# Reordering the turn from batch 0 to batch 1 in a Strassen MLP behind block-recurrent attention: what VectorE and ScalarE do first

## The chip, the cores and the metric

The kernel runs on one core of a Trainium2 chip. The metric is device time in microseconds, as the median of several executions; lower is better. A profile of one execution shows every instruction of five engines: TensorE (PE, its weight loads PEld), VectorE (DVE), ScalarE (ACT), GpSimd (POOL) and SyncE (SP), which issues the transfers (DMA). Each engine works through its own list of instructions in the order of the program; the order is written by hand here, and the waits between engines follow from the data and the buffers.

## The reference

Two parts, all in fp32. First attention between a sequence and a small state, for 8 batches and 8 heads of width 64; then an MLP with a quick GELU on all 8 x 544 tokens.

```python
B, H, S, Ns, D = 8, 8, 512, 32, 64
scores = scale * x @ state.T                 # (B, H, S, Ns); scale = 1/sqrt(D)
xread  = softmax(scores) @ state             # x reads the state
scores2 = scale * state @ x.T                # (B, H, Ns, S)
sread  = softmax(scores2) @ x                # the state reads x
y = concat([xread, sread], axis=2)           # (B, H, S + Ns, D) -> (4352 tokens, 512)
h = y @ w_in                                 # 512 -> 2048
g = h / (1 + exp(-1.702 * h))
out = g @ w_out                              # 2048 -> 512
```

## The kernel before

The inputs x and the weights come as 64-bit words, and the kernel turns the weights into fp32 itself, 128 rows at a time (a row block: 16 of w_in, then 16 of w_out): a mask on VectorE, a clamp of the exponent by two activations on ScalarE, then four more operations on VectorE. ScalarE's clamp for later row blocks is asked for ahead (`powers_to`).

```python
def round_a(i):                      # mask (DVE, L216) and clamp
    if i not in power: mask(i)
    ...
    nc.scalar.activation(out=sc.bitcast(FP32), in_=sc, func=AF.Relu, bias=edge[0], scale=-8.0)   # L227
    nc.scalar.activation(out=sc, in_=sc.bitcast(FP32), func=AF.Relu, bias=edge[1], scale=-1.0)   # L228

def round_b(i, ahead, follows):      # needs the clamp of i
    nc.vector.scalar_tensor_tensor(sc, hi, -0x80000000, sc, ...)                                 # L245
    powers_to(ahead)
    nc.vector.scalar_tensor_tensor(dst, lo, 2.0**-32, dst.bitcast(I32), ALU.mult, ALU.add)       # L248
    if follows and i + 1 in raw: fraction(i + 1)                                                 # L234
    nc.vector.scalar_tensor_tensor(dst, dst, 2.0**-20, sc.bitcast(FP32), ALU.mult, ALU.mult)     # L252

def round_to(n, ahead=AHEAD):
        ...
        round_b(i, min(i + 1 + ahead, i + 2 if i >= nin else nin), ...)   # nin = 16: from there on w_out
```

The down-projection (g @ w_out) is done by Strassen's scheme in Winograd's form: seven products P1 to P7 in place of eight, at the cost of sums of blocks. The sums of the left side are S1 = A21 + A22, S2 = S1 - A11, S4 = A12 - S2 and S3 = A11 - A21; those of the right side (the weights) are T1 = B12 - B11, T2 = B22 - T1, T4 = B21 - T2 and T3 = B22 - B12. For batch 0 this runs while w_out is still arriving, a loop over 8 pairs of row blocks, with the rest of batch 1's up-projection (`up_x`) between:

```python
rest = list(range(2 * nper, NF))         # f = 8 .. 15 of batch 1's up-projection
for i in range(HF):                      # HF = 8
    round_to(nin + 2 * i + 2)
    if i == 0:
        pair(i, "P1", "P2")
        for b in (1, 0):
            for g in range(NG):
                att_eT(b, g)             # four transposes on PE into two banks, copied by ACT
        round_to(nin + 4)
        att_sread(1); att_sread(0)       # the states' reads
        att_M(1, 2, True); att_M(1, 3)
        ...
        pair_sums(i)
        att_srT(0); att_srT(1)
        ps7["P4"], up_bank = (psH.tile(...) for k in (4, "up"))
    else:
        pair_sums(i); pair(i, "P1", "P2")
    if i > 1:
        up_x(1, rest.pop(0), bank=up_bank)      # matmuls, then the gelu on ACT (L549)
    late()                                      # P6 P5 P7 P3 P4 of pair i
    if i == HF // 2:
        load_state(2); load_x_squares(2)
```

Behind the loop come the sums for the batches 1 to 7. These use Strassen's scheme twice: each of the products (256 x 1024 by 1024 x 256) of the outer level is made of seven smaller ones, so every weight block needs sums of its own (three, `low_sums`) and one in place (`low_third`). The sums of three blocks are kept in SBUF in turn (`low_made`), all are stored in DRAM (`low_keep`) and loaded again for later batches. `low_away` makes them in a passing room (tag xT, one buffer) and stores them.

```python
def low_sums(t, rooms):                  # each step needs the one before
    return [(T_of, v) for v in ((t1, b12, b11), (t2, b22, t1), (t4, b21, t2))]

low_away(6, B22)
low_made(5, T1, 1)
for u in range(NU - 2): s12(1, u, S)     # S1, S2 of batch 1, two of four quarters
                                         # batch 0's epilogue: 7 additions, out by DMA
nc.scalar.copy(k1, ps7["P1"]); tt(osb, ps7["P2"], k1, ALU.add); ...
for f in rest:                           # f = 14, 15
    up_x(1, f, bank=up_bank)
...                                      # two copies on ACT: the T2, T4 of pairs 0 to 3
s12(1, NU - 2, S)
low_third(T1)
for u in range(NU - 1): s3(1, u, S)
low_away(3, T3); low_third(T3)
turn_x(2)                                # four 32x32 transposes of batch 2's x
low_made(2, T2, 0)
s12(1, NU - 1, S); s3(1, NU - 1, S)
for b in range(1, B):
    ...
    ahead = {"P1a": [(low_third, (B22,)), (low_third, (T2,)), (low_away, (4, T4)), (low_third, (T4,))]}   # b == 1
    ...
    strassen_two(b, out_of(b), hooks, a4)
```

In `strassen_two` hooks with names run between the products; for batch 1 P1 and P2 are plain, and P5, P6, P3, P7, P4 are the two-level ones:

```python
product(bank(0), A_of(0, 0), B11, "P1"); nc.scalar.copy(k1, bank(0))       # hooks P1a, P1b after each half
for i in range(3):
    sums1[i](); sums2[i]()               # VectorE: sums of S1, of S2
third_of(S1)
product(bank(1), A_of(0, 1), B21, "P2"); tt(osb, bank(1), k1)              # hooks P2a, P2b; bank(1) = bank_o[1]
first = {...: s4(u) at P5.1, .2, .5, .6; third_of(S2) at P5.3}             # for later batches sums2 too
strassen_low(left_of(S1, *r), (T1 ...), [h0, h1, bank_o[1]], p5, at)       # P5

def strassen_low(left, right, bank, R, at):       # x, y, z are the three banks
    product(x, a11, b11, True); nc.scalar.copy(y, x);     at(1)   # L700
    product(z, s1, t1, True);   nc.scalar.copy(c22, z);   at(2)   # L703
    product(y, s2, t2);         nc.scalar.copy(c12, y);   at(3)   # L706
    product(x, a12, b21);       nc.scalar.copy(c11, x);   at(4)   # L709
    product(y, a21, t3);        add(c22, y, c22);         at(5)   # L696
    product(z, s4, b22);        add(c12, z, c12);         at(6)
    product(y, a22, t4);        nc.scalar.copy(c21, y);   at(7)   # L718
```

At batch 1 the hooks P2a and P2b also hold the start of batch 2's attention: scores, two products with w_in (`att_M`), two transposes and two maxima on VectorE (P2a), and the two exps on ScalarE (`att_s_exp`, P2b), which write to the room with the tag xT.

Of the kernel before, what the change touches and what calls it, by code (L numbers as in the profile page):

```python
# [20 lines left out]
def kernel(  # L21
# [71 lines left out]
    def att_ps(shape, name):  # L93
        return psA.tile(shape, FP32, tag="att", name=name)
# [142 lines left out]
    def round_b(i, ahead, follows):  # L237


        if i not in begun:  # L240
            fraction(i)
        dst = begun.pop(i)
        lo, hi = words(i)
        sc = power.pop(i)
        nc.vector.scalar_tensor_tensor(sc, hi, -0x80000000, sc, ALU.bitwise_and, ALU.bitwise_or)  # L245
        powers_to(ahead)

        nc.vector.scalar_tensor_tensor(dst, lo, 2.0**-32, dst.bitcast(I32), ALU.mult, ALU.add)  # L248
        del raw[i]
        if follows and i + 1 in raw:  # L250
            fraction(i + 1)
        nc.vector.scalar_tensor_tensor(dst, dst, 2.0**-20, sc.bitcast(FP32), ALU.mult, ALU.mult)  # L252
# [19 lines left out]
    def round_to(n, ahead=AHEAD):  # L272

        nin = NFC * NPR
        while done["b"] < min(n, len(PIECES)):
            i = done["b"]
            powers_to(i + 1)
            round_b(i, min(i + 1 + ahead, i + 2 if i >= nin else nin), i >= nin or i + 1 < nin and (i + 1 < n or i >= NPR))
            done["b"] += 1
            while done["b"] > NPR and done["load"] < len(PIECES) and before(done["load"]) < done["b"]:  # L280
                load_weights(done["load"] + 1)
# [183 lines left out]
    def att_M(b, c, spare=False, banks=None):  # L465

        m = mpool.tile([P, NG, FC], FP32, tag=f"M{turns['M'] % NFC if b < 2 else c}", name=f"M_{b}_{c}")
        turns["M"] += 1
        A[b]["M", c] = m
        name = f"M_{b}_{c}_"  # L470
        ps = banks or [
            psH.tile([P, FC], FP32, tag="h", name=name + str(g)) if spare else att_ps([P, FC], name + str(g)) for g in range(NG)
        ]
        by_state(b, ps, lambda rows, j: w_in[c][rows, j])
        for g in range(NG):
            nc.scalar.copy(m[:, g], ps[g])  # L476
# [16 lines left out]
        t = A[b]["eT"][:, g].rearrange("p c q -> p (c q)")  # L493
        nc.vector.transpose(t, t)

    def att_eT(b, g):

        a = A[b]
        if g == 0:
            a["eT"] = apool.tile([P, NG, SCH, P], FP32, tag="e1" if b else "eT", name=f"eT_{b}")  # L500
        ps = att_ps([P, SCH, P], f"eT_{b}_{g}")
        for c in range(SCH):
            nc.tensor.transpose(ps[:, c], a["e2"][g][0][:, P * c : P * (c + 1)], ident)
        nc.scalar.copy(a["eT"][:, g], ps)
# [216 lines left out]
    def strassen_two(key, dst, hooks, a4):  # L721
# [129 lines left out]
        if key == 1:  # L851
            for i in range(3):
                sums1[i]()
                sums2[i]()
            third_of(S1)
            product(bank(1), A_of(0, 1), B21, "P2")
            tt(osb, bank(1), k1)
        else:
            o, h0, h1 = low_banks()
            own2 = {2: sums1[:1], 4: sums1[1:2], 5: sums1[2:], 6: [lambda: third_of(S1)]}  # L860
            lowly("P2", left2, B21, low_a, [h0, o, h1], osb, own2)
            low_load(2, 0)
            tt(osb, osb, k1)
# [6 lines left out]
        hook("P2")  # L870
        first = {i + 1: [lambda u=u: s4(u)] for i, u in zip((0, 1, 4, 5), range(NU))}
        first[3] = [lambda: third_of(S2)]
        if key > 1:
            first[1].insert(0, sums2[0])
            first[2].append(sums2[1])
            first[4] = sums2[2:]
        o, h0, h1 = low_banks()

        def at(i):
# [403 lines left out]
    def low_made(k, t, i):  # L1283

        for fn, args in low_sums(t, (low_a, low_b)[i]):
            fn(*args)
        low_keep(k, turn_rooms[i])
# [49 lines left out]
    def pair(i, *names):  # L1337

        f = ORDER[i]
        a11, a12, a21, a22 = a_of(f)  # L1340
        s1, s2, s4 = s_of(i) if i >= 0 and names[0] not in ("P1", "P2") else (None,) * 3
        t = t24(i) if s1 is not None else None
        for name in names:
            lhs, rhs = {
                "P1": lambda: (a11, B11[:, f]),
                "P2": lambda: (a12, B21[:, f]),
                "P5": lambda: (s1, T1[:, f]),
                "P6": lambda: (s2, t[:, 0]),
                "P7": lambda: (a21, B12[:, f]),
                "P3": lambda: (s4, B22[:, f]),  # L1350
                "P4": lambda: (a22, t[:, 1]),
            }[name]()
            for r in range(2):
                nc.tensor.matmul(  # L1354
                    ps7[name][:, HN * r : HN * (r + 1)], lhs[:, P * r : P * (r + 1)], rhs,
                    start=(i == 0 and r == 0), stop=(i == HF - 1), skip_group_check=True,
                )

    def late():

        pair(i, "P6", "P5", "P7", "P3", "P4")
        if i % 2:
            u = ORDER[i] // 2
            free.append(G.pop((0, u)))
            G.pop((0, HF // 2 + u))

    rest = list(range(2 * nper, NF))
    for i in range(HF):
        round_to(nin + 2 * i + 2)
        if i == 0:  # L1370
            pair(i, "P1", "P2")
            for b in (1, 0):
                for g in range(NG):
                    att_eT(b, g)
            round_to(nin + 4)
            att_sread(1)
            att_sread(0)
            att_M(1, 2, True)
            att_M(1, 3)
            t_room.append(pieces(apool.tile([P, NG, SCH * P], FP32, tag="eT", name="t_room_1"), 2, 2))  # L1380
            s4_room = pieces(apool.tile([P, NG, NB * Ns], FP32, tag="e1", name="s4_room"), 2, 2)
            pair_sums(i)
            att_srT(0)
            att_srT(1)
            ps7["P7"], ps7["P3"] = (att_ps([P, FC], f"down_{k}") for k in (7, 3))
            ps7["P4"], up_bank = (psH.tile([P, FC], FP32, tag="h", name=f"down_{k}") for k in (4, "up"))
# [4 lines that stand above are left out]
            up_x(1, rest.pop(0), bank=up_bank)  # L1391
        late()
        if i == HF // 2:
            load_state(2)
            load_x_squares(2)

    low_away(6, B22)
    low_made(5, T1, 1)
    for u in range(NU - 2):
        s12(1, u, S)  # L1400

    k1, k2, t01, k3 = (v[:, j] for v in (s_room, s4_room) for j in range(2))
    osb = opool.tile([P, 2, HN], FP32, tag="osb", name="osb_0_00")
# [7 lines left out]
    tt(osb, ps7["P2"], k1, ALU.add)  # L1411
    put_out(0, 0, osb)
    tt(k2, ps7["P6"], k1, ALU.add)
    tt(t01, ps7["P5"], k2, ALU.add)
    tt(k3, ps7["P7"], k2, ALU.add)
    tt(k1, ps7["P7"], t01, ALU.add)
# [2 lines left out]
    put_out(0, 1, t01)  # L1419
    tt(k3, ps7["P4"], k3, ALU.add)  # L1420
    put_out(1, 0, k3)
    for f in rest:
        up_x(1, f, bank=up_bank)
    for i, t in enumerate(t_room):
        nc.scalar.copy(sums[:, 2, 2 * S * i : 2 * S * (i + 1)], t.rearrange("p n k t -> p (n k t)"))
    s12(1, NU - 2, S)
    low_third(T1)
    for u in range(NU - 1):
        s3(1, u, S)
    low_away(3, T3)  # L1430
    low_third(T3)
    turn_x(2)
    low_made(2, T2, 0)
    s12(1, NU - 1, S)
    s3(1, NU - 1, S)

    for b in range(1, B):
        if b > 1:
            ahead = {"P1.1": [(up_strassen(b, S, *parts_x(b), A[b]["sums"]), ())]}
            if b == 2:  # L1440
                ahead["P1.5"] = [low_sums(B21, low_a)[2], (low_keep, (1, turn_rooms[0]))]
                ahead["P1.6"] = [(low_third, (B21,))]
        else:
            ahead = {
                "P1a": [(low_third, (B22,)), (low_third, (T2,)), (low_away, (4, T4)), (low_third, (T4,))]
            }
        if b + 1 < B:
            hooks = hooks_next(b + 1)
        else:

            steps, left, right = sr_sums()
            order = (
                ("P5.6", 2), ("P6.1", 3), ("P6.3", 6), ("P6.4", 7), ("P7.5", 8), ("P7.6", 9), ("P4.1", 16, 17), ("P4.5", 18, 19),
            )
            hooks = {name: [steps[i] for i in n] for name, *n in order}
            hooks["P3.7"] = [(low_third, (T1,))]
            beside = steps[10:16] + [(low_third, (t,)) for t in (B11, B21, T2, T3, T4, B22)]
            ahead["P2.1"] = [steps[i] for i in (0, 1)]
            ahead["P2.3"] = [steps[i] for i in (4, 5)]
        for name, first in ahead.items():  # L1460
            hooks[name] = first + hooks.get(name, [])
        a4 = {}

        at = hooks.setdefault("run", [])
        k = 3 if b + 1 < B else 0
        at[k:k] = [(low4_load, (a4,))]
        strassen_two(b, out_of(b), hooks, a4)
        if b + 2 < B:
            load_state(b + 2)
            load_x_squares(b + 2)  # L1470
# [35 lines left out]
```

## Time and profile before

| | |
|---|---|
| median of 3 runs | 710.29 us (709.15 to 710.42) |
| span in the profile | 708.5 us |
| TensorE busy | 684.5 us (97%) |
| VectorE busy | 573.5 us (81%) |
| ScalarE busy | 321.1 us (45%) |
| HBM traffic | 86.5 MB, 122 GB/s over the span |

In the profile an instruction appears with its engine, the line of the kernel, what it writes and reads (names of the program), and the idle time of its engine before it with what ended that. fp32 matmuls appear as two records each. A busy share is an average over all stages: the stage in which the engine stood still has to be looked up by its time. The part that matters here lies between 60 and 215 us: the loop over pairs to about 145, the turn from batch 0 to batch 1 to about 182 (the end of P5), and the other products of batch 1 to 211.

### The profile page before, as it was taken

How to read it: one execution, taken by the hardware profiler on the slowest of the kernel's cores; microseconds unless marked ns; L12 is line 12 of the kernel's file. 1: busy time of each engine (PE TensorE's matmuls, PEld its weight loads, DVE VectorE, ACT ScalarE, POOL GpSimd, SP SyncE). 2: the span in 40 equal slices, each digit the busy share in tenths (PEclk: the TensorE clock that was granted, in tenths of full speed). 3: DMA queues.
4: the chain of work that ended last, by engine and by line, in shares of the span. 5: the costliest groups of instructions: out<-in, count | busy, mean ns of one | idle time of the engine just before them, and what ended most of it. 6: DMA issues, size and time to landing. Idle time of an engine off the chain costs nothing.

```text
span 708.5 us, 13782 instructions
## 1 busy us (share of the span) xinstructions
PE 684.5 (97%) x5357; PEld 580.1 (82%) x5359; DVE 573.5 (81%) x1226; ACT 321.1 (45%) x704; POOL 0.8 (0%) x8
## 2 busy tenths in 40 slices
PE   7989999995999999999999999999999999999996
PEld 3433587773998799889999889889988998999995
DVE  6999979999697979697869887888878895887540
ACT  5687833313236543555346433652375336512420
POOL 0000000000000000000000000000000000000000
PEclk9999999997999999999999999999999999999999
DMA  8921326154525285516641474237433640241001
GB/s 224 369 80 63 106 91 148 63 192 150 163 76 124 81 262 150 109 35 194 204 105 34 128 247 125 42 107 237 148 65 105 211 149 31 59 144 66 16 1 31
DMA packets 106321, 87.41 MB, mean 123 GB/s; under 512 B 64784, under 2 KB 85776, under 8 KB 106256
## 3 DMA queue, kind: packets, MB, share of 16 engines
q1 hardware_dynamic: 106256, 86.53, 41.7%
q8 instruction: 43, 0.70, 0.4%
q14 instruction: 22, 0.18, 0.1%
HBM read 68.94 MB, written 17.56 MB: 122 GB/s over the span
## 4 chain that ended last, share of the span: by engine, by line
PE 85%; DVE 8%; ACT 3%; DMA 2%; issue 1%; SPq 0%; DVEq 0%; ACTq 0%
PE low L691 27%; PE o L691 15%; PE o L1111 13%; PE upx L1111 5%; PE h L546 5%; PE M L329 4%; PE o L1354 3%; PE o L588 2%; PE down L1354 2%; PE upw L1111 2%; PE o L329 1%; PE down_up L546 1%; PE sr L517 1%; PE warm L127 1%; DVE low L1281 1%; PE upx_sr L1111 1%
## 5 line engine op out<-in xcount | busy, mean ns | idle before, releaser
L691 PE MATMUL low<-w_out,g 128*128 128x128 f32 x416 | 54.3, 276 | 0.0
L691 PEld LDWEIGHTS low<-w_out,g 128*128 128x128 f32 x416 | 50.5, 192 | 4.5 <-issue 3.4
L1111 PE MATMUL o<-ta,M 128*128 128x256 f32 x192 | 49.9, 382 | 0.0
L1111 PE MATMUL upx<-aT,M 128*128 128x256 f32 x192 | 49.3, 379 | 0.0
L691 PE MATMUL low<-low,g 128*128 128x128 f32 x336 | 43.3, 275 | 0.0
L691 PEld LDWEIGHTS low<-low,g 128*128 128x128 f32 x336 | 40.3, 192 | 0.1
L1111 PEld LDWEIGHTS o<-ta,M 128*128 128x128 f32 x192 | 35.5, 190 | 6.0 <-ACT g L1157 1.6
L1111 PEld LDWEIGHTS upx<-aT,M 128*128 128x128 f32 x192 | 36.0, 190 | 4.6
L691 PE MATMUL low<-sums,later 128*128 128x128 f32 x280 | 36.1, 276 | 0.0
L1117 ACT ACTIVATE g<-o 128x512 f32<-128x512 f32 (+1 forms) x56 | 31.3, 559 | 10.2 <-PE o L1111 10.2
L476 ACT COPY M<-M 128x512 f32<-128x512 f32 x59 | 30.7, 597 | 11.6 <-PE M L329 11.6
L691 PEld LDWEIGHTS low<-sums,later 128*128 128x128 f32 x280 | 34.0, 194 | 0.1
L329 PE MATMUL M<-w_in,stT 64*32 64x512 f32 x472 | 31.9, 594 | 0.0
L1111 PE MATMUL o<-ta,ms 128*128 128x256 f32 x120 | 30.8, 379 | 0.0
L546 PE MATMUL h<-aT,M 128*128 128x512 f32 x64 | 28.7, 599 | 1.4 <-ACT M L476 1.4
L691 PE MATMUL o<-low,spare_M 128*128 128x128 f32 x160 | 22.2, 283 | 8.1 <-DVE osb L747 8.1
L227 ACT ACTIVATE low<-low,edge 128x512 f32<-128x512 int32 x30 | 21.6, 719 | 13.9 <-DVE low L216 13.8
L1117 ACT ACTIVATE g<-g 128x512 f32<-128x512 f32 (+1 forms) x28 | 16.8, 600 | 23.4 <-DVE g L1120 23.4
L691 PEld LDWEIGHTS o<-low,spare_M 128*128 128x128 f32 x160 | 20.3, 199 | 8.3 <-DVE osb L747 8.3
L546 PEld LDWEIGHTS h<-aT,M 128*128 128x128 f32 x64 | 11.8, 190 | 18.3 <-issue 12.0
L1157 ACT COPY g<-o 128x512 f32<-128x512 f32 (+1 forms) x28 | 15.5, 554 | 24.4 <-PE o L1111 24.4
L1111 PEld LDWEIGHTS o<-ta,ms 128*128 128x128 f32 x120 | 22.8, 190 | 3.1
(285 smaller groups left out, 1656.7 us busy)
## 6 DMA issues: line engine op xcount, KB each, us to landing
low<-low SPq DMA_DIRECT2D x108, 256.0 KB, 2.7
low<-low SPq DMA_DIRECT2D x11, 768.0 KB, 4.3
later<-in_moe_w_out_dram SPq DMA_DIRECT2D x16, 512.0 KB, 3.4
w_out<-in_moe_w_in_dram SPq DMA_DIRECT2D x12, 512.0 KB, 5.9
xsq<-in_x_dram SPq DMA_DIRECT2D x96, 64.0 KB, 2.4
xn<-in_x_dram SPq DMA_DIRECT2D x12, 512.0 KB, 4.5
out_dram<-osb SPq DMA_DIRECT2D x15, 256.0 KB, 2.2
out_dram<-later SPq DMA_DIRECT2D x14, 256.0 KB, 2.1
```

The costliest lines, as they stand in the source:

```text
L127: nc.tensor.matmul(ps, zeros[:, :P], zeros, start=True, stop=True)
L227: nc.scalar.activation(out=sc.bitcast(FP32), in_=sc, func=AF.Relu, bias=edge[0], scale=-8.0)
L329: nc.tensor.matmul(ps[g][st], A[b]["stT"][rows, st], rhs(rows, j), start=True, stop=True)
L476: nc.scalar.copy(m[:, g], ps[g])
L517: nc.tensor.matmul(ps[st, g], e, v, start=(c == 0), stop=(c == SCH - 1),)
L546: nc.tensor.matmul(hps, lhs[i], rhs[i], start=(i == 0), stop=(i == n - 1))
L588: nc.tensor.matmul(ps[:, r], lhs[f][:, P * r : P * (r + 1)], rhs[:, f], start=(first and r == 0 and f == 0), stop=(f == HF - 1), skip_grou ...
L691: nc.tensor.matmul(ps, lhs[f], rhs[:, f], start=(first and f == 0), stop=(f == QF - 1), skip_group_check=True)
L1111: nc.tensor.matmul(ps[:, k], lhs[i][:, o : o + P], rhs[i], start=(first and k == 0 and i == 0), stop=(i == n - 1), skip_group_check=True,)
L1117: nc.scalar.activation(out=dst, in_=src, func=AF.Gelu_apprx_sigmoid)
L1157: nc.scalar.copy(c12, Y(u))
L1354: nc.tensor.matmul(ps7[name][:, HN * r : HN * (r + 1)], lhs[:, P * r : P * (r + 1)], rhs, start=(i == 0 and r == 0), stop=(i == HF - 1), s ...
```

## The change

Five things are changed in order or place; the arithmetic is the same.

1. From w_out on, a row block's clamp is asked for two blocks ahead, not one.
2. In turn 0 the transposes of batch 1's attention go to the other pair of banks (`psH`), `att_M(1, 2)` goes before the states' reads, and P6 of pair 0 before their transposes.
3. Behind the loop the sums of B22 and T1, and those of S1 and S2, are made in turns, so that no step needs the one just before it. Of batch 1's own sums, S1's come first; those of S2 move into P5, as in later batches. The stored sums of T2 and T4 go behind them, into the hooks of P2, and the thirds of B22, T3 and T4 into P6 and P3.
4. The last block of `up_x` goes to a bank of its own (`bank_o[2]`).
5. `low_third(T1)` goes into the epilogue, between steps that need each other.

It is meant to bring what the first two-level product (P5) waits for to the front of VectorE's list, and to put off what is wanted later.

```diff
-            round_b(i, min(i + 1 + ahead, i + 2 if i >= nin else nin), ...)
+            round_b(i, min(i + 1 + ahead, i + 3 if i >= nin else nin), ...)
...
-    def att_eT(b, g):
+    def att_eT(b, g, spare=False):
-        ps = att_ps([P, SCH, P], f"eT_{b}_{g}")
+        ps = psH.tile([P, SCH, P], FP32, tag="h", name=name) if spare else att_ps([P, SCH, P], name)
...
             for i in range(3):
                 sums1[i]()
-                sums2[i]()
+                hook(f"S1.{i}")
             third_of(S1)
...
-        if key > 1:
-            first[1].insert(0, sums2[0])
-            first[2].append(sums2[1])
-            first[4] = sums2[2:]
+        first[1].insert(0, sums2[0])
+        first[2].append(sums2[1])
+        first[4] = sums2[2:]
...
-        pair(i, "P6", "P5", "P7", "P3", "P4")
+        pair(i, *(("P6",) if i else ()), "P5", "P7", "P3", "P4")
...
-                    att_eT(b, g)
+                    att_eT(b, g, b == 1)
             round_to(nin + 4)
+            att_M(1, 2, True)
             att_sread(1)
             att_sread(0)
-            att_M(1, 2, True)
             att_M(1, 3)
...
             pair_sums(i)
+            pair(i, "P6")
             att_srT(0)
...
-    low_away(6, B22)
-    low_made(5, T1, 1)
-    for u in range(NU - 2):
-        s12(1, u, S)
+    room = away(6)                                   # the xT room
+    turns_of(low_sums(B22, low_parts(room)), low_sums(T1, low_b))
+    low_keep(6, room)
+    low_keep(5, turn_rooms[1])
+    turns_of(s12_steps(0), s12_steps(1))
+    low_away(3, T3)
...
     tt(k2, ps7["P6"], k1, ALU.add)
+    low_third(T1)
     tt(t01, ps7["P5"], k2, ALU.add)
...
-    for f in rest:
-        up_x(1, f, bank=up_bank)
+    for f, bank in zip(rest, (up_bank, bank_o[2])):
+        up_x(1, f, bank=bank)
...
-    s12(1, NU - 2, S)
-    low_third(T1)
-    for u in range(NU - 1):
-        s3(1, u, S)
-    low_away(3, T3)
-    low_third(T3)
+    turns_of(s12_steps(2), s12_steps(3))
+    s3(1, NU - 1, S)
     turn_x(2)
-    low_made(2, T2, 0)
-    s12(1, NU - 1, S)
-    s3(1, NU - 1, S)
...
-                "P1a": [(low_third, (B22,)), (low_third, (T2,)), (low_away, (4, T4)), (low_third, (T4,))]
+                "P2a": [(low_away, (4, T4))],
+                "P2b": [(low_made, (2, T2, 0)), (low_third, (T2,))],
+                "P6.4": [(low_third, (B22,))],
+                "P3.1": [(low_third, (T3,))],
+                "P3.2": [(low_third, (T4,))],
             }
+            for u in range(NU - 1):
+                ahead[f"S1.{u}"] = [(s3, (1, u, S))]
```

More of the change, by code (lines that the diff above doesn't have):

```diff
@@ L277, in round_to @@
             powers_to(i + 1)
-            round_b(i, min(i + 1 + ahead, i + 2 if i >= nin else nin), i >= nin or i + 1 < nin and (i + 1 < n or i >= NPR))
+            round_b(i, min(i + 1 + ahead, i + 3 if i >= nin else nin), i >= nin or i + 1 < nin and (i + 1 < n or i >= NPR))
             done["b"] += 1
@@ L500, in att_eT @@
             a["eT"] = apool.tile([P, NG, SCH, P], FP32, tag="e1" if b else "eT", name=f"eT_{b}")
-        ps = att_ps([P, SCH, P], f"eT_{b}_{g}")
+        name = f"eT_{b}_{g}"
+        ps = psH.tile([P, SCH, P], FP32, tag="h", name=name) if spare else att_ps([P, SCH, P], name)
         for c in range(SCH):
@@ L1395, with turns_of, away, s12_steps @@
             load_x_squares(2)
-    low_away(6, B22)
-    low_made(5, T1, 1)
-    for u in range(NU - 2):
-        s12(1, u, S)
+    def turns_of(*lists):
+        for step in zip(*lists):
+            for fn, args in step:
+                fn(*args)
+    def away(k):
+        room = apool.tile([P, NPR, S], FP32, tag="xT", name=f"away_{k}")
+        return room.rearrange("p j t -> p (j t)")[:, : 3 * FC]
+    def s12_steps(u):
+        (a11, a21), (_, a22) = quarters(1, u, S), quarters(1, HF // 2 + u, S)
+        s1, s2 = S1[:, 2 * u : 2 * u + 2, :HS], S2[:, 2 * u : 2 * u + 2, :HS]
+        return [(tt, (s1, a21, a22, ALU.add)), (tt, (s2, s1, a11))]
+    room = away(6)
[4 more added lines that the diff above has]
+    low_away(3, T3)
     k1, k2, t01, k3 = (v[:, j] for v in (s_room, s4_room) for j in range(2))
```

## The prediction, on record before the changed kernel was run

> **What bounds the kernel now.** I read the page first: TensorE is busy for 97% of the span and VectorE for 81%, so a change can only pay where TensorE stands still. The row of slices shows one such place behind the start, the slice with PEclk 7. The table of windows cuts it out (columns: window, length, then busy time of PE, PEld, DVE, ACT and POOL, granted clock, DMA share, GB/s), and the view of waits names who waited there.
>
> ```profile
> PE 684.5 (97%) x5357; PEld 580.1 (82%) x5359; DVE 573.5 (81%) x1226; ACT 321.1 (45%) x704; POOL 0.8 (0%) x8
> PEclk9999999997999999999999999999999999999999
> ...
> 165.00:170.00 5.00, 1.79 (x13) 1.48 (x11) 4.93 (x9) 1.00 (x3) 0.00 (x0) 0.89 0.55 154
> 170.00:175.00 5.00, 0.08 (x1) 0.08 (x1) 4.93 (x11) 2.82 (x4) 0.00 (x0) 0.50 0.63 213
> 175.00:180.00 5.00, 5.00 (x27) 5.00 (x28) 1.75 (x3) 1.41 (x6) 0.00 (x0) 0.59 0.57 109
> ...
> PE o L691 <- DVE osb L747: 8.1, 1, 8.1
> DVE low L245 <- ACT low L228: 5.2, 1, 5.2
> ACT L386 <- DMA low<-away: 5.0, 1, 5.0
> ```
>
> TensorE waits once, for 8.1 us, while VectorE is full. The other two waits belong to the same story, and the timeline of single instructions shows how (start, length, engine, line, operands, idle time before it and what ended it):
>
> ```profile
> 101.57 0.60 ACT L549 ACTIVATE g<-down_up 128x512 f32<-128x512 f32 x1 [8.43 <-PE down_up L546]
> 102.06 0.71 ACT L227 ACTIVATE low<-low,edge 128x512 f32<-128x512 int32 x1
> ...
> 103.56 0.69 DVE L245 SCALAR_TENSOR_TENSOR low<-later,low 128x512 int32<-128x512 int32 x1 [5.24 <-ACT low L228]
> ...
> 147.05 1.98 PE L546 MATMUL down_up<-low,M 128*128 128x512 f32 x4 [0.69 <-ACT g L549]
> 165.73 1.05 PE L691 MATMUL low<-sums,later 128*128 128x128 f32 x8
> 174.92 2.07 PE L691 MATMUL o<-low,spare_M 128*128 128x128 f32 x8 [8.13 <-DVE osb L747]
> ...
> 171.01 1.28 ACT L386 ACT_TABLE_LOAD   x1 [5.01 <-DMA low<-away]
> ...
> 174.17 0.69 DVE L747 TENSOR_TENSOR osb<-o,g 128x512 f32<-128x512 f32 x1
> ```
>
> At 165.73 the first product of P5 (S1 T1) of batch 1 runs, at 174.92 the second. Its bank o was P2's bank, and comes free when VectorE has read P2 out of it (osb, 174.17). That add is late only because VectorE works its list in order: it is full from 103.56 to 174.9, with a list 34.9 us long between the last pair's sums (end 139.23) and the osb add. The chain of waits agrees: from 132 to 174 it runs on VectorE almost alone.
>
> **What the Trainium skill says.** "TensorE: Matmul & The Clock Gate" (Part 1: The HAM clock gate) has TensorE at half rate after an idle window of about 3.4 us, and full again after about as long of work. The trace agrees roughly: in windows of 1 us the clock is 1.00 until 168, 0.95, then 0.50 until 179, so it fell some 2.2 us after the last matmul and rose 4.2 us after the next. Same page (Architectural detail): ScalarE and VectorE are strict FIFO. That is the wait at 103.56: the clamp (L227, L228) had its mask ready at 96.8 but stood behind a gelu (L549) that waited for TensorE. "VectorE: DVE Perf Modes" (Two Vector instructions with no wait between them) says an instruction that isn't held starts before the last has drained. Here 128x512 subtractions come every 0.60 us when independent, every 0.70 to 0.72 when each needs the one before it. "ScalarE: Activation LUTs" (What ACT_TABLE_LOAD costs) gives 1283 ns; the trace shows 1.28 us at 171.01.
>
> **The change part by part.**
>
> *Clamps two ahead.* Each row block's clamp now stands before the gelu of the same turn, so the idle 5.24 us at 98.3 goes, and VectorE runs 5.2 us ahead. Later clamps then stand behind the gelu of the turn before, and are ready when wanted (gelu at 109.3, clamps done at 111.3 and 112.7; VectorE wants them near 111.3 and 113.9). Part is given back to a transfer. With w_out's row blocks numbered 0 to 15 as they are loaded, block 14 is loaded behind 16 loads of x (issued from 114.55 for 8.66 us), so its issue comes 10.4 us after block 9 is read (112.95 to 123.32). It lands 3.4 us later, at +13.8; its mask, now made with block 12, is reached at +11.9 (the dense list from 112.95 to 124.86). That stalls VectorE for some 1.9 us: net lead 3.4 us, so the last pair sums end at 135.8. TensorE's loop itself doesn't shorten; from 88 to 145 it has no gap.
>
> *State reads in other banks.* The four transposes no longer wait for each other's banks (0.24 and 0.19 us of waits), but a clamp (two activations, 1.4 us) now stands before the gelus whose banks they need, and M(1,2) and P6 fill the rest. I make it 0.2 us earlier at P5 of pair 0 (88.43 to 88.2).
>
> *Gelus in two banks.* up_x(1,15) gets bank_o[2], which the first epilogue add empties. With VectorE at 135.8: six sums of B22 and T1 in turns 3.65, four of S1 and S2 2.45 (to 141.9), T3's stored sums 2.06. Their room is the one that B22's go out of: issued at 138.9, 768 KB move in some 2.8 us (before: issued 141.40, traffic from 142 to 144.1), so free near 141.7, no stall. The osb add then ends at 144.7. up_x(1,14) runs from 144.3, up_x(1,15) from 146.05, without the 0.69 us. Batch 1's P1 begins at 147.75 instead of 148.88: 1.1 us.
>
> *VectorE's list before the osb add.* From the timeline: 0.60 us an operation in turns, 2.06 for three chained. B22 and T1 3.65, S1/S2 of u=0,1 2.45, T3 2.06, epilogue with T1's third 4.85, S1/S2 of u=2,3 2.45, one S3 0.60, turning x 2.40, S1's three sums in turns with three S3 3.70, S1's third 0.60, T4 2.06, two transposes 1.20, two maxima 1.50, T2 2.06, its third 0.60. Together 30.2 us instead of 34.9: the three sums of S2 and the thirds of B22, T3 and T4 go behind it (6 x 0.60 = 3.6), the turns save 1.1. It starts at 166.0 and ends at 166.7, against 174.86.
>
> *P5.* TensorE needs 16.85 us from P1 to P5 as before (148.88 to 165.73), so P5 begins at 164.6. Second product: from 166.75 (the bank), 0.89 long. Third: needs ScalarE's copy of the first, which stands behind the exps. T4's sums end near 160.7, their way out takes 4.35 (166.65 to 171.0 before, beside x), to 165.1; table load 1.28; two exps 1.95; copy 0.3: 168.6. Third product from 168.65 to 169.55, four more at 0.89: P5 ends at 173.1. Before it ended at 182.38. **That is 9.3 us**, of which about 2.2 us is the slow clock from 174.9 to 179.1 (4.2 us at half rate) and the rest waiting. Idle pieces of 1.25 and 1.0 us remain; they are shorter than the 2.2 us after which the clock fell.
>
> *Given back.* P5 takes three S2 sums more (with its own work 5.4 us of VectorE in 8 us: fits). B22's third falls where VectorE was idle for 2.11 us. T3's and T4's land in P3, from where VectorE was full until 211; P7's last product had 0.34 us to spare behind an add. So up to 1.2 us there, say 0.9. Remaining: 8.4 us. Behind it TensorE waits for 1.6 us in all to the end, so what is won stays. For small waits I haven't seen I take 0.6 off: 7.8 us, **702.5 us**.
>
> **Rivals.** (1) ScalarE takes VectorE's place: the exps wait for the stored T4, and if the x loads slow that transfer by 2 us, P5's third product waits longer, the clock falls, and 3 to 4 us are lost: about 706. The 5.0 us wait in the profile is for this; against it, the transfer starts 4 us before P5, not with it. (2) Transfers stall VectorE: row blocks 14 and 15 behind the x loads, or the shared room of B22 and T3. If 1.8 us more is lost there, T4's sums end at 162.5, the copy comes at 170.4, and the gain is 6 us: 704.3. (3) VectorE is full behind P5 too, and the moved work comes back there (P3, P7, and the first products of batch 2's up-projection): 2 to 3 us, 704.5. For: no idle time from 189.9 to 211. Against: it comes to 1.2 us of work. (4) Nothing remains in the way: row block 14 is there in time, P5 follows P2 at once: 10.5 to 11 us, 699.5. (5) The eT copies behind the early clamp delay the loop by over 1 us: 703.5.
>
> **Range and chances.** Most rivals cost 1 to 4 us of 8, and one adds 3, so 8 times in 10 it should lie between 699.5 and 706.5. 2% is 14.2 us, more than all that TensorE loses here (8.1 + 2.2 + 0.7 = 11.0 us), so faster by over 2% is next to excluded: 0.02. Slower by over 2% would need a new wait as long, 0.02; within 2%, 0.96.
>
> **What would show it.** Right: no idle time on VectorE near 98 to 103; a wait of about 2 us for a load of w_out near 120; up_x(1,15) right behind up_x(1,14); the wait of P5's second product at 1 to 2 us, the third's on ScalarE; PEclk without a slice of 7; VectorE idle time gone in P5, TensorE waits below 1 us in P7. Wrong: if P5 begins later than 166, the list in front of P2 is longer than I made it; if the 8 us go and the time stays above 706, they came back later as waits for VectorE between P3 and batch 2's up-projection; if the clock still falls there, the rest of the wait was over 2 us.

## Result: 703.09 us, and the profile after

The changed kernel takes 703.09 us (median of 4 runs, 701.66 to 705.08), the kernel before 710.36 us beside it: a ratio of 0.9901, 95% interval 0.9872 to 0.9931. Measured again (e11): 703.47 us, 0.9916 (0.9904 to 0.9929). The prediction was 702.5 us, within 699.5 to 706.5.

First the page and the table of windows of the changed kernel, the same rows as before, then its view of waits between 66 and 180 us (who waited for whom: us in total, times, longest):

```profile
PE 683.3 (98%) x5357; PEld 578.5 (83%) x5359; DVE 571.7 (82%) x1226; ACT 320.7 (46%) x704; POOL 0.8 (0%) x8
PEclk9999999999999999999999999999999999999999
...
165.00:170.00 5.00, 2.11 (x17) 1.73 (x16) 4.97 (x9) 3.85 (x7) 0.00 (x0) 1.00 0.99 365
170.00:175.00 5.00, 5.00 (x48) 5.00 (x47) 3.35 (x11) 0.80 (x3) 0.00 (x0) 1.00 0.84 183
175.00:180.00 5.00, 5.00 (x48) 5.00 (x46) 3.50 (x10) 1.58 (x5) 0.00 (x0) 1.00 0.91 316
...
ACT L386 <- DMA low<-away: 3.6, 1, 3.6
...
DVE low L216 <- DMA later<-in_moe_w_out_dram: 2.3, 1, 2.3
...
PE o L692 <- DVE osb L748: 2.0, 1, 2.0
...
PE low L692 <- ACT low L701: 0.9, 1, 0.9
```

The slice with a clock of 7 is gone, and between 170 and 180 TensorE is full where it had worked 5.1 us of 10, most of it at half rate. One wait of 8.1 us has become two, 2.0 for VectorE and 0.9 for ScalarE. A wait for a transfer has appeared on VectorE. The timeline shows where each lies:

```profile
122.38 0.43 DVE L216 TENSOR_SCALAR low<-later 128x512 int32<-128x512 int32 x1 [2.25 <-DMA later<-in_moe_w_out_dram]
...
145.83 1.88 PE L547 MATMUL o<-low,M 128*128 128x512 f32 x4
...
164.41 1.05 PE L692 MATMUL low<-sums,later 128*128 128x128 f32 x8
167.44 1.16 PE L692 MATMUL o<-low,spare_M 128*128 128x128 f32 x8 [1.98 <-DVE osb L748]
169.51 1.16 PE L692 MATMUL low<-low,spare_M 128*128 128x128 f32 x8 [0.92 <-ACT low L701]
...
186.24 1.16 PE L692 MATMUL low<-low,g 128*128 128x128 f32 x8 [0.39 <-DVE later L697]
```

I use one mark throughout: the first matmul of batch 2's up-projection (`upx`), where the part that the change touches is over. It stood at 210.60 us and stands at 202.96: 7.64 us earlier. From there to the end both kernels run the same list; it took 497.9 us before and 496.9 after, and between these and 499.5 in the traces of the other runs.

### The profile page after: what moved, and what is told of

The parts are those of the page before. It is cut to its first block, busy times and chain, and to the rows that moved or that the text cites. A ratio compares the mean times of both kernels' runs of the same rounds, so it can differ in the third digit from the quotient of the medians.

```text
span 699.9 us, 13779 instructions
## 1 busy us (share of the span) xinstructions
PE 683.3 (98%) x5357; PEld 578.5 (83%) x5359; DVE 571.7 (82%) x1226; ACT 320.7 (46%) x704; POOL 0.8 (0%) x8
## 4 chain that ended last, share of the span: by engine, by line
PE 88%; DVE 5%; ACT 4%; DMA 2%; issue 1%; SPq 0%; DVEq 0%; ACTq 0%
PE low L692 27%; PE o L692 14%; PE o L1111 13%; PE upx L1111 5%; PE h L547 4%; PE o L1354 4%; PE M L329 4%; PE down L1354 3%; PE o L589 2%; PE upw L1111 2%; PE down_up L547 2%; PE o L741 1%; PE o L329 1%; PE warm L127 1%; PE upx_sr L1111 1%; DMA out_dram<-osb_sr 1%
## 5 line engine op out<-in xcount | busy, mean ns | idle before, releaser
L1111 PE MATMUL o<-aT,m 128*128 128x256 f32 x96 | 24.6, 379 | 0.0
L692 PEld LDWEIGHTS o<-w_out,g 128*128 128x128 f32 x160 | 19.4, 192 | 5.0 <-issue 5.0
```

Of the source, the lines that this page charges most:

```text
L692: nc.tensor.matmul(ps, lhs[f], rhs[:, f], start=(first and f == 0), stop=(f == QF - 1), skip_group_check=True)
L1111: nc.tensor.matmul(ps[:, k], lhs[i][:, o : o + P], rhs[i], start=(first and k == 0 and i == 0), stop=(i == n - 1), skip_group_check=True,)
```

## The experiments

All with medians, the kernel before measured beside each. "Wait" is TensorE's for the osb add ahead of P5's second product; "mark" is the time just defined.

| run | us | before beside it | ratio (95%) | wait | mark |
|---|---|---|---|---|---|
| kernel before | | 710.36 | | 8.1 | 210.60 |
| changed kernel | 703.09 | 710.36 | 0.9901 (0.9872 to 0.9931) | 2.0 | 202.96 |
| e1 clamps only | 706.72 | 709.42 | 0.9958 (0.9942 to 0.9973) | 4.4 | 208.49 |
| e2 banks only | 708.96 | 709.42 | 0.9991 (0.9984 to 0.9998) | 8.2 | 208.98 |
| e3 list only | 707.55 | 709.42 | 0.9968 (0.9954 to 0.9983) | 3.9 | 207.94 |
| e4 x behind weights | 700.39 | 709.42 | 0.9866 (0.9850 to 0.9881) | 0.2 | 200.55 |
| e5 T4 early | 699.62 | 709.56 | 0.9853 (0.9841 to 0.9866) | 0.2 | 200.30 |
| e6 thirds in P5 | 699.29 | 709.56 | 0.9848 (0.9835 to 0.9861) | 0.2 | 199.49 |
| e7 first clamps late | 697.75 | 709.56 | 0.9829 (0.9816 to 0.9841) | 0.2 | 198.73 |
| e8 before, kept busy | 709.10 | 709.56 | 0.9994 (0.9985 to 1.0002) | 1.0 | 208.52 |
| e9 before again | 710.13 | 710.16 | 1.0004 (0.9996 to 1.0013) | 8.1 | 210.74 |
| e10 kept busy again | 709.24 | 710.16 | 0.9990 (0.9981 to 0.9999) | 1.0 | 208.69 |
| e11 changed again | 703.47 | 710.16 | 0.9916 (0.9904 to 0.9929) | 2.3 | 204.01 |

**e1: the clamps alone**, on the kernel before.

```diff
-            round_b(i, min(i + 1 + ahead, i + 2 if i >= nin else nin), ...)
+            round_b(i, min(i + 1 + ahead, i + 3 if i >= nin else nin), ...)
```

> The kernel before with the clamps two ahead and nothing else. Theory A (P5 waits for VectorE's list, and the list is as long as the work in it): the 5.24 us idle near 98 go, 2.25 us of a wait for row block 14 come, so the list ends 3.0 us earlier, the osb add at about 171.8 instead of 174.86, TensorE's wait in P5 is about 5.1 us; that is still over 2.2 us, so the clock falls as before and its 2.1 us stay lost. Batch 2's up-projection begins at about 207.6 instead of 210.60; time 3.0 us below the kernel before. Rival B (the clamps' lead is lost to the transfer of row block 14, VectorE being held by the loads): no gain, below 1 us.

2.7 us faster, and rival B falls. VectorE's timeline has 0.18 us of waiting where there were 5.24, and a new wait for row block 14:

```profile
104.34 0.69 DVE L245 SCALAR_TENSOR_TENSOR low<-later,low 128x512 int32<-128x512 int32 x1 [0.18 <-ACT low L228]
122.43 0.43 DVE L216 TENSOR_SCALAR low<-later 128x512 int32<-128x512 int32 x1 [1.88 <-DMA later<-in_moe_w_out_dram]
...
171.17 0.69 DVE L747 TENSOR_TENSOR osb<-o,g 128x512 f32<-128x512 f32 x1
```

The osb add begins 3.0 us earlier, as expected (174.17 before). But the mark moved by 2.1 us, not 3.0: the clock stayed low for 6.1 us after TensorE went on. Half of that, 3.0 us, is the work lost by estimate, where the first trace had 2.1. The early clamp also costs something: it stands before the last gelus of batch 0, and TensorE's loop ends 0.77 us later than before (0.1 of that is there at 65.5 us already, ahead of what the edit touches).

**e2: TensorE's own gains alone**: `att_eT` in the other banks, `att_M(1, 2)` and P6 moved, and

```diff
-    for f in rest:
-        up_x(1, f, bank=up_bank)
+    for f, bank in zip(rest, (up_bank, bank_o[2])):
+        up_x(1, f, bank=bank)
```

> The kernel before with only what TensorE itself gains: state reads in other banks, M(1,2) and P6 moved, the last block of the up-projection in bank_o[2]. Theory A: P1 of batch 1 begins 0.4 to 1.3 us earlier, but P5's second product still waits for the osb add at 174.9, so the wait grows to about 9 us and the time stays the same within 0.5 us. Rival C (TensorE's own gaps count): 1 us or more faster.

0.5 us faster; theory A had "the same within 0.5", rival C 1 us or more. The wait kept its length, where theory A saw it grow: both ends moved. The loop ended 1.1 us earlier (up_x(1,14) at 143.39 instead of 144.49), and VectorE with it: its last pair sum begins at 137.80, not 138.90. In the kernel before VectorE is tied to TensorE's loop through the gelus that its clamps stand behind, so what TensorE gains in the loop VectorE gains too. The mark moved by 1.6 us, the medians by 0.5. About 0.5 us of the 1.6 is chance: the clock stayed low for 3.1 us after TensorE went on, not 4.2, which is 1.55 us of lost work by estimate, not 2.1. The traced execution has a mean granted clock of 0.995; of the other 19 only two have it, and 14 have 0.990 or 0.991. So theory A was right on the time, and wrong on the osb add, which it kept at 174.9.

**e3: the order of VectorE's list alone**: the changed kernel with the two parts above undone (what is left are parts 3 and 5 of the change).

> The changed kernel with clamps one ahead and without the bank changes: only the order of VectorE's list differs from the kernel before. Theory A: the list begins at 139.2 as before and takes 30.5 us, so the osb add ends near 170.4; TensorE waits 3.8 us, ScalarE's copy is there near 172.4, and the clock may still fall at 169 (up to 2 us more). P5 ends at 177 to 179 instead of 182.4, time 3.5 to 5.4 us below the kernel before. If it were the order alone (rival D), it would bring nearly all of the change's 7.6 us.

1.9 us faster, below the range; at the mark 2.7. The wait is 3.9 us as expected (3.8), the osb add begins at 170.13, but the clock fell all the same. The windows of e3:

```profile
165.00:170.00 5.00, 2.00 (x14) 1.68 (x12) 4.86 (x10) 0.79 (x1) 0.00 (x0) 0.94 0.89 271
170.00:175.00 5.00, 4.13 (x18) 3.86 (x18) 4.43 (x8) 3.12 (x7) 0.00 (x0) 0.50 0.85 286
175.00:180.00 5.00, 5.00 (x41) 5.00 (x41) 2.39 (x9) 0.80 (x3) 0.00 (x0) 0.88 0.91 229
```

The waiting is 4.3 us shorter, but 5.4 us at half rate cost 2.7 us of work (2.1 before), a wait of 0.4 us appears in P3 (worth 0.65 at the mark, as e6 shows), and the loop ended 0.2 us later: 2.8 us are left by this account, and 2.7 are seen. Rival D falls: neither the order nor the clamps alone bring much over a third of the change. Alone the clamps, the banks and the list bring 2.7, 0.5 and 1.9 us, 5.0 together; in one kernel 7.3. At the mark they bring 2.1, 1.6 and 2.7, 6.4 together against 7.6. In the trace of each of the three kernels the clock falls, in the two of the changed one it doesn't.

**e4: x behind the weights**, on the changed kernel.

```diff
-        if i == HF // 2:
+        if i == HF // 2 + 1:
             load_state(2)
             load_x_squares(2)
```

> The changed kernel with batch 2's state and x loads asked for one pair later, behind the last two row blocks of w_out. Theory A: the 2.25 us wait for row block 14 goes, the osb add ends about 2 us earlier (165.3), P5's second product waits 0.3 us or less, the third about 0.9 us for ScalarE; P5 ends near 171.8 instead of 174.1 and batch 2's up-projection begins 2 to 2.4 us earlier than 202.96. Rival E (ScalarE's exps, not VectorE, hold P5): the second wait grows to what the first loses, and less than 1 us is won.

The wait for row block 14 is gone, and both waits of P5 shrink together, so rival E falls:

```profile
165.57 1.16 PE L692 MATMUL o<-low,spare_M 128*128 128x128 f32 x8 [0.21 <-DVE osb L748]
167.11 1.16 PE L692 MATMUL low<-low,spare_M 128*128 128x128 f32 x8 [0.38 <-ACT low L701]
```

The mark is 2.4 us earlier. The median is 2.7 us less, or 1.8 us if each is counted from the kernel before beside it. It is also steadier: 699.64 to 700.80, where the changed kernel spread over 3.4 us. e11 shows one reason and points to a second.

**e11: the changed kernel again.**

> The changed kernel once more, for its interval and a second trace. Median 702 to 704; batch 2's up-projection at 203.0 within 0.3 us, clock 1.00 throughout P5.

The mark missed its 0.3 us: it stands at 204.01. VectorE's wait for row block 14 took 3.23 us this time, not 2.25, and that shift of 1 us passes through the osb add to the end:

```profile
123.44 0.43 DVE L216 TENSOR_SCALAR low<-later 128x512 int32<-128x512 int32 x1 [3.23 <-DMA later<-in_moe_w_out_dram]
...
168.51 1.16 PE L692 MATMUL o<-low,spare_M 128*128 128x128 f32 x8 [2.33 <-DVE osb L748]
```

The second reason is the clock. Each execution has its mean granted clock on record, traced or not. Of the changed kernel's nine executions, four have 0.998 to 1.000 (the two traced ones 1.000) and took 701.66 to 703.09 us; five have 0.995 to 0.997 and took 703.47 to 705.08. The 43 executions of e4 to e8 and e10 have 0.998 to 1.000, but for one at 0.997; where the trace shows 0.998 (e4, e6), the slow stretch lies in the last 4 us of the span. So in about half of its executions the changed kernel probably lost some of its clock after all. In which stage isn't shown, as none of these five was traced.

**e5: T4's stored sums earlier**, in a room that the exps don't need; on e4.

```diff
     s3(1, NU - 1, S)
+    low_made(4, T4, 0)
     turn_x(2)
...
-                "P2a": [(low_away, (4, T4))],
```

> e4_x_behind_weights with T4's stored sums made earlier (before x is turned) in the room of T2's, not in the room that the exps need. Theory A: the exps no longer wait for that transfer (1.3 us in e4), so ScalarE's copy is there when P5's first product is done, and the 0.38 us wait of the third product goes; the wait of the second (0.21 us) stays, the list is equally long. Batch 2's up-projection begins about 0.4 us earlier, time 0.4 us less than e4. Rival F (what sits on the path now is VectorE alone, ScalarE has slack): the second product's wait grows by what the third's loses, nothing is won.

The third product no longer waits, and the second's wait didn't grow: rival F falls. The mark is 0.6 us nearer the end of the loop (up_x(1,14) to mark: 56.54 before, 55.92 now); the medians differ by 0.8 us, about their spread.

**e6: the thirds of T3 and T4 in P5**, on e5.

```diff
-                "P3.1": [(low_third, (T3,))],
-                "P3.2": [(low_third, (T4,))],
+                "P5.7": [(low_third, (T3,)), (low_third, (T4,))],
```

> e5_t4_early with the thirds of T3 and T4 moved from P3 (where VectorE is full) to the end of P5 (where it stood idle). If the 0.39 us wait of TensorE in P3 is what the change gave back, it goes, and the time is 0.4 us less than e5. If P3's wait is due to VectorE's own work there, it stays near 0.4 us.

TensorE's 0.4 us wait in P3 is gone, so it was what the change gave back there. The mark moved by 0.8 us, 0.65 of it behind the end of the loop. That is more than the wait of 0.39: a wait is counted from the end of the product before, which is 1.06 us long, while products that need not wait begin every 0.89 us. The median fell by 0.3 us, which is within the spread: shown in the trace, not in the times.

**e7: the first clamps late**, on e6.

```diff
-            i + 3 if i >= nin else nin
+            (i + 3 if i >= nin + 4 else i + 2) if i >= nin else nin
```

> e6_thirds_in_p5 with the clamps one ahead up to row block 3 and two ahead only from block 4, so that block 4's clamp stands behind the gelus and the eT copies again. Theory: the early clamp cost 0.67 us in the states' reads (e1 against the kernel before), hidden in the changed kernel by the other banks; taken off, up_x(1,14) begins 0.5 to 0.7 us earlier, and since P5 now waits for hardly anything, 0.3 to 0.6 us of it remain in the time. Rival G: VectorE's list then ends too late and the second product's wait takes all of it.

up_x(1,14) begins 0.76 us earlier (0.17 of it is there at 65.5 us already), the wait in P5 is still 0.24 us, and the mark is 0.76 us earlier: all of it arrives, so rival G falls. The medians differ by 1.5 us, twice as much; why isn't shown. At 697.75 us this is the fastest version, 1.7% below the kernel before.

**e8, e9, e10: what the slow clock costs.** The kernel before with matmuls that only keep TensorE busy while it waits; their results are overwritten.

```diff
         product(x, a11, b11, True)
+        for n in range(32):                    # only in P5 of batch 1
+            nc.tensor.matmul(y, a11[n % QF], b11[:, n % QF], start=True, stop=True, ...)
```

> The kernel before, with 32 more matmuls into the bank of P5's third product while it waits for the osb add (about 7.1 us at 0.2234 each; their results are overwritten by ScalarE's copy). If the slow clock is due to the idle time and costs about 2.1 us, the clock stays at 1.00, the wait shrinks to about 1 us at unchanged end (174.9), and batch 2's up-projection begins 2.1 us earlier than 210.60; time 2.1 us less. If the clock falls for another reason, or the cost is counted elsewhere, the time stays the same.

```profile
166.50 7.31 PE L701 MATMUL low<-sums,later 128*128 128x128 f32 x64
174.79 1.16 PE L691 MATMUL o<-low,spare_M 128*128 128x128 f32 x8 [0.98 <-DVE osb L749]
```

In the trace it comes out as written: clock 1.00 in every window, the second product where it was, the mark 2.08 us earlier (0.13 of it is there before P5). The times say less: 0.5 us, and the interval reaches 1.0002, so that it may be nothing. Two more traces were to tell why.

> The kernel before once more, for a second trace. e8 moved the start of batch 2's up-projection by 2.1 us in its trace, but the medians by 0.5 us only. Either the slow clock costs 2.1 us in the first trace and less in most executions (theory: it depends on where the clock's window lies, so this trace shows another loss, between 1 and 3 us, as e1 and e3 did with 3.0 and 2.6), or the stages behind differ by 1 to 2 us between executions of one kernel (rival: from batch 2 on to the end 497.9 us in the first trace; a value off by 0.5 us or more speaks for it). Time the same within 0.3 us.

> e8 once more. Theory: batch 2's up-projection begins at 208.5 again (within 0.3 us of the start of the loop), the clock stays at 1.00; median 709.1 within 0.5 us. If the time from there to the end is over 498 us here, the stages behind give back what was won.

The kernel before lost 2.25 us to the clock in its second trace. The traced executions are no exception in this: beside the runs e1 to e11 the kernel before has a mean granted clock of 0.990 to 0.995 in every execution, and the 27 executions of e8 and e10 have 0.997 to 1.000. e10 won its 2.05 us at the mark again, and gave them back behind it: from the mark to the end it took 499.5 us, e9 497.2. Its view of waits names the place:

```profile
PE low L691 <- DMA low<-low: 1.8, 1, 1.8
...
PE o L691 <- DMA low<-low: 0.5, 1, 0.5
```

These are the loads of stored sums in later batches. They come to nothing in e9 and to 0.8 us in e8. So the rival of e9 holds: from the mark to the end two traces of one kernel differ by 0.7 us (497.9 and 497.2, the kernel before) and by 1.6 (497.9 and 499.5, e8 and e10). Over both sets the filler brings 0.5 and 0.9 us; how much of a microsecond won in P5 arrives in the median is open to within 1 us for single parts. Whether a load is later because TensorE is earlier was not tried.

## Why the prediction was right, point by point

- **What bounds:** shown. The osb add, and with it VectorE's list, held P5: e1 and e3 each shortened it by its own amount, and the wait ended with the add each time.
- **Clamps:** the 5.24 us are gone; the wait for row block 14 was predicted at 1.9 us and is 2.25 and 3.23 in two traces. The last pair sums end at 136.18 instead of 135.8. This term was sized 0.35 us too small in the first trace and 1.3 in the second; e4 shows that the whole wait was worth 2.4 us at the mark.
- **State reads:** "0.2 us earlier" is 0.37 (P5 of pair 0 at 88.06). It is the sum of two larger things: about 0.7 us lost by the early clamp (e1, taken off in e7) and about 1 us won by the banks (e2).
- **up_x(1,15):** right behind its neighbour, at 145.83 against 146.05; P1 at 147.55 against 147.75.
- **The list:** 30.5 us to the osb add's start (136.18 to 166.70) where I had 30.2; the difference is the wait for the shared room, 0.30 us, that I had as none.
- **P5:** the second product begins at 167.44 (predicted 166.75), the third at 169.51 (168.65), and P5 ends at 174.08 (173.1): 8.3 us, not 9.3. ScalarE was named rightly as the holder of the third; its wait is 0.92 us (1.0).
- **Given back:** a wait in P3, where it was expected, of 0.39 us instead of 0.9. With the 0.6 us held back for small waits the sum came out 0.2 us above the mark's 7.64: an error of 1 us in P5 and a margin of nearly 1 us too many cancelled. That the number came out so close is luck.
- **The clock:** didn't fall in the two traces. The reason that I gave, that the waits are shorter than the 2.2 us after which it fell, is not shown: in e11 a wait of 2.33 us left it at 1.00, and in five of nine executions the mean clock speaks for a fall (e11). The traces may have had luck here: see below.
- **Not seen:** that the clamps, the banks and the list need each other. I took the clock's 2.1 us as won because the remaining waits were short; with any one of the three alone it still fell.
- **Rivals:** (2) came true in small, with 0.35 us more for row block 14 and 0.30 for the shared room, and (3) with the wait in P3. (5), the early clamp, cost about 0.7 us in e1, which the other banks hid. (1) didn't come: ScalarE holds P5 for 0.9 us only. What (4) described is reached by e4 to e7, 11.9 us earlier at the mark than the kernel before.

## What to carry to other kernels

Where one engine works through a list in order, ask of the one wait that matters which entries stand in front of it and are not needed for it; here 3.6 us of 34.9 could go behind and 5.2 us of idle time lay in front. An item that an in-order engine does for another one (here the clamp) should stand before anything in its list that waits for a third, unless what it pushes back is itself waited for: the first clamps did better late (e7). When an engine is made earlier, look at once at the transfers that are issued behind others: the next wait, for row block 14, was one of those, and moving sixteen small loads behind two large ones brought a third as much again as the whole change.

## What the runs showed of the hardware

- TensorE's clock fell 2.1 to 4.5 us after the end of the last matmul (2.1 and 2.4 in two traces of the same kernel, 2.4 in e3, 3.6 in e1, 4.5 in e2) and rose 3.1 to 6.1 us after the next one began. The work lost so, by estimate half of the time at half rate, was 1.55 us (e2), 2.1 and 2.25, 2.7 (e3) and 3.0 (e1). A shorter wait can thus lose more than a long one: e1 with 4.4 us of waiting lost 3.0, e2 with 8.2 us lost 1.55.
- The time at half rate came in whole pieces. It lasted 10.24 us in both traces of the kernel before (168.90 to 179.14 and 169.17 to 179.41), and 6.83 us in e1 (171.17 to 178.00), e2 (170.10 to 176.93) and e3 (169.41 to 176.24): three and two times 3.41. The edges are worked out from windows of half a microsecond; the first two lines are of the kernel before, the last two of e2. A granted clock of 0.90 stands there for 0.40 us at full and 0.10 us at half rate, if there is nothing between.

```profile
168.50:169.00 0.50, 0.00 (x0) 0.00 (x0) 0.50 (x2) 0.00 (x0) 0.00 (x0) 0.90 1.45 319
179.00:179.50 0.50, 0.50 (x6) 0.50 (x6) 0.00 (x0) 0.00 (x0) 0.00 (x0) 0.86 0.96 189
...
170.00:170.50 0.50, 0.00 (x0) 0.00 (x0) 0.50 (x2) 0.50 (x1) 0.00 (x0) 0.60 1.09 387
176.50:177.00 0.50, 0.50 (x5) 0.50 (x4) 0.00 (x0) 0.00 (x0) 0.00 (x0) 0.57 0.98 186
```

- "TensorE: Matmul & The Clock Gate" of the Trainium skill (Part 1: The HAM clock gate) has a window of about 3.4 us that runs freely. These lengths fit it; where the window lies against the wait is then chance. The window that ended with the fall need not have been idle throughout: in the kernel before, the 3.41 us up to 168.90 hold 1.3 us of matmuls and 2.1 of waiting. Two waits of 2.0 and 0.9 us with 1.15 us of work between (the changed kernel; 2.3 and 0.9 in e11) left the clock at 1.00 in both traces. But up to 2.3 us of this waiting fit into 3.41 us, so by this estimate the clock can fall there too, if the window lies badly.
- One kernel's traces differ by up to 1.6 us in stages where TensorE is otherwise full (e8 and e10, from the mark to the end); its waits for loads of stored sums differ by 1.5 us there (0.8 and 2.3). Gains below 1 us are better read at a mark in the trace than from medians of a few runs, though the mark of a single trace holds chance too (0.5 us in e2, 1 us in e11).
